# A third chunk's layer norm without TensorE transposes, in a kernel that adds a long convolution to a two-layer MLP

## The chip, the cores and the metric

The kernel runs on one core of a Trainium2 chip. The metric is device time in microseconds; the kernel before took 358.84 us, the median of three runs (358.47 to 358.85). Engines are named as in the profile: PE (TensorE matmuls), PEld (TensorE weight loads), DVE (VectorE), ACT (ScalarE), POOL (GpSimd) and SP (SyncE, here only a queue of DMAs).

## The reference

All tensors have 2048 positions and 448 channels. The input x is layer-normed to xn; the result is x plus two branches.

```python
def A(xn, k, v, shift_k, ssm_k, ssm_D):
    k_shift = sum(k_pad[:, t:t + S] * shift_k[:, 3 - t] for t in range(4))   # causal, 4 taps
    kv = k_shift * v
    y = irfft(rfft(pad(kv), 2 * S) * rfft(pad(ssm_k), 2 * S))[:S]            # long causal convolution
    return xn * (y + kv * ssm_D)

def B(xn, w1, b1, w2):
    h = xn @ w1 + b1                       # 448 -> 1792
    return (h * tanh(softplus(h))) @ w2    # Mish, 1792 -> 448

out = x + A(layernorm(x), k, v, shift_k, ssm_k, ssm_D) + B(layernorm(x), w1, b1, w2)
```

## The kernel before, in words

**The MLP sets the pace.** The 2048 positions are cut into eight chunks of 256. The 1792 hidden channels are seven pairs of 128, so that there are 56 (chunk, pair) items. Item i has two slots of an order that is written out by hand: in slot 2i its first matmul (`g1_mm`, L512, 22 TensorE instructions), and in slot 2i+1 ACT's Mish and its split (`mish`, `split`: L520, L84, L85) together with the second matmul (`g2_mm`, L544 to L546, 12 instructions) of item i-2. Float32 operands are split into a high part, which ACT casts, and a low part, which DVE subtracts: XH and XL for xn, `ach` and `acl` for the activation, `w1h`/`w1l` and `w2h`/`w2l` for the weights. A chunk's two accumulators of the second matmul (`pg2`, two buffers in PSUM, one for each half of the chunk) are added to x by DVE at the chunk's end (`g2_evac`, L551), and only then can the next chunk's second matmul begin.

**The convolution is laid between.** It is a transform in two stages, by small matmuls. In the stretch that the change touches, eight pieces of the kernel of the convolution ("h") and eight of kv go through the first stage: a visit `f1_mm` (L146, PE) reads one piece and writes the PSUM tiles `pq` and `pr`, ACT copies one half to `st` (L152), DVE folds the halves (L156, two instructions) and ACT's queue stores `st` to DRAM (L167). The kv visits stand in slots 24, 29, 34, 39, 44, 50, 55 and 59. Ahead of each, DVE makes the piece from k and v (`taps`: L189, L192, L194 products, L199 sums, L202 the product with v); one product of four is POOL's (L182).

**Layer norm has two forms.** For chunks below NT (0 to 3), `ln_load` and `ln_stats` load x and take mean and variance (L406, L409, L412, POOL's power L415), POOL normalizes (L419, L423), and `ln_T` has PE transpose the result to PSUM (L464, four instructions for each half of a chunk), from which ACT and DVE split it (L476, L474). For chunks from NT on, x is also loaded in a transposed copy (`xT_load`, L434); `nt_stats` stores mean and power to DRAM (L442), `nt_row` (L445) reads them back spread over all partitions, DVE subtracts and multiplies (`nt_norm`, L451, two instructions a half), and `nt_split` (L458, L459) splits from SBUF. The row read back overwrites the identity matrix of the transposes. The table `NT_HOW` gives for each such chunk the slots, counted from the start of the chunk before it, of its load ("q"), transposed load ("x"), statistics, the flush of the statistics, and the rows, norms and splits of its two halves.

**What sets the order.** `at` puts a step in front of a slot's matmuls, `after` behind them. Each engine runs its own instructions strictly in that order, SP's DMA issues too, so that an issue which waits holds up those behind it. Small DVE steps can be put on a list (`drip`) that is taken from between other DVE work, or emptied at once; `ln_T` of a first half empties it.

Of the kernel before, what the change touches and what calls it, by code (L numbers as in the profile page):

```python
# [17 lines left out]
NP = NF // 2  # L18
# [5 lines left out]
G2_LAG = 2  # L24
# [5 lines left out]
I2_AT = {100: ((6, 7, 0, 1), 92, (95, 97, 98, 99), (0, 2, 0, 1)),  # L30
         108: ((2, 3, 4, 5), 101, (104, 105, 106, 107), (0, 1, 0, 1))}
LATE = 2
NT = 4
NT_AT = {"q": -5, "x": -1, "stats": -2, "flush": 0, "row": (4, 8), "norm": (7, 10), "split": (8, 11)}
NT_SOON = dict(NT_AT, row=(4, 5), norm=(4, 7), split=(6, 8))
NT_HOW = {c: NT_SOON for c in (3, 4, 7)}
NT_HOW[5] = dict(NT_AT, q=-8, stats=-4, flush=-2)
WARM_N = (448, 448, 448)
FILL_N = (224, 112, 96)
# [3 lines left out]
def tile_kernel(ctx: ExitStack, tc, q, qT, k, v, sk, hT, sD, w10, w1, w2, c_fib, c_g, c_gi, c_i2, out):  # L43
# [20 lines left out]
    E = dp.tile([NJ * 4, 64, D], F32, name="E")  # L64
    MR = {c: dp.tile([2, CH], F32, name="MR") for c in range(NT, NCHUNK)}

# [8 lines left out]
    def rs(c):  # L75
        return rstd[:, 2 * c:2 * c + 2] if c < NT else mv[:, 2 * c:2 * c + 2, 1]

# [26 lines left out]
    def dv(n=1):  # L104
        for _ in range(n):
            if drip:
                drip.pop(0)()
# [4 lines left out]
    def at(slot, fn, *args):  # L112
        plan.setdefault(int(slot), []).append((fn, args))

    def after(slot, fn, *args):
        plan2.setdefault(int(slot), []).append((fn, args))
# [278 lines left out]
    def xn_tile():  # L395
        return mp.tile([128, 4, CH], F32, name="xn", bufs=1)

    def ln_parts(c):
        st = mp.tile([128, 2, 6], F32, name="bst", bufs=2)
        ve = mp.tile([128, 2], F32, name="ve", bufs=2)  # L400
        if c < NT:
            XN[c] = xn = xn_tile().rearrange("p a b -> p (a b)").rearrange("p (j d) -> p j d", j=2)
        eng = nc.gpsimd if 0 < c < NCHUNK - 1 else V

        def stats(jj):
            V.bn_stats(st[:, jj], Q[c][:, jj])  # L406

        def aggr(jj):
            V.bn_aggr(mv[:, 2 * c + jj], st[:, jj])  # L409

        def eps(a, b):
            V.tensor_scalar(ve[:, a:b], mv[:, 2 * c + a:2 * c + b, 1], EPS, None, op0=ALU.add)  # L412

        def power(a, b):
            nc.gpsimd.tensor_tensor(rs(c)[:, a:b], ve[:, a:b], mhalf[:, a:b], op=ALU.pow)  # L415

        def norm(jj):
            j = 2 * c + jj
            eng.tensor_scalar(xn[:, jj, :D], Q[c][:, jj], mv[:, j, 0:1], rs(c)[:, jj:jj + 1],  # L419
                              op0=ALU.subtract, op1=ALU.mult)  # L420

        def tail(a, b, copy=eng.tensor_copy):
            copy(xn[:, a:b, D:], xn[:, a:b, D - 64:D])  # L423

        return stats, aggr, eps, power, norm, tail, ve
# [52 lines left out]
    def ln_T(c, jj):  # L478
        if jj == 0:
            dv(len(drip))  # L480
            x_tiles(c)
        p = pg()
        transposes(c, jj, p)
        for lo in range(2):
            x_split(c, jj, p, lo)
# [73 lines left out]
    def mlp_slot(s):  # L559
# [3 lines left out]
        if half == 0:  # L563
            if i < n:
                c, p = pairs[i]
                if c + 1 < NT:
                    if p == 0:
# [8 lines left out]
        else:  # L576
            if i < n:
                c, p = pairs[i]
                if p == NP - 2 and c + 1 < NT:
                    ln_T(c + 1, 0)  # L580
# [39 lines left out]
    for p in range(NP):  # L620
        if p >= 3:
            at(max(2 * p - 5, 0), w1_load, p)
        if p == 1 or p > 2:
            at(2 * p - 2, w1_split, p)
        p and at(2 * p + (1 if p < 5 else 0), w2_load, p)
        at(2, w2_split, p) if p == 0 else after(2 * (p + G2_LAG) - 1, w2_split, p)

    at(OCT_AT[0], regroup)
    for o in range(NO):
# [34 lines left out]

    for c in range(NT, NCHUNK):
        at_ = NT_HOW.get(c, NT_AT)
        b = 2 * NP * (c - 1) + (1 if c == NT else 0)
        at(b + at_["q"], ln_load, c)
        at(b + at_["x"], xT_load, c)
        at(b + at_["stats"], nt_stats, c)  # L670
        at(b + at_["flush"], lambda: dv(len(drip)))
        for jj in range(2):
            at(b + at_["row"][jj], nt_row, c, jj)
            after(b + at_["norm"][jj], nt_norm, c, jj)
            after(b + at_["split"][jj], nt_split, c, jj)
# [28 lines left out]
    stats, aggr, eps, power, norm, tail, ve = ln_parts(0)  # L704
# [120 lines left out]
```

## Time and profile before

| | before |
|---|---|
| median of 3 runs | 358.84 us (358.47 to 358.85) |
| profiled execution | 359.38 us |
| its span, first to last instruction | 357.6 us |
| outside the span | 1.78 us |
| granted TensorE clock | 0.998 |
| PE busy | 352.0 us, 98% |
| DVE busy | 269.1 us, 75% |
| ACT busy | 156.8 us, 44% |
| POOL busy | 76.5 us, 21% |

The share of DVE is a mean over unlike stages: from 61.9 to 169.1 us, while the kv pieces are made, it is busy for 103.0 of 107.2 us. The chain that ended last runs through PE for 86% of the span. A row of the timeline gives start, duration, engine, line and operation, and in brackets for how long the engine sat idle before it and what ended that. Instructions of PE and DVE overlap their successors a little, so the time that an instruction costs a queue that never idles is the distance between starts, not the printed duration.

### The profile page before, as it was taken

The numbers are of one execution on the slowest core, as the hardware profiler recorded it, in microseconds if no ns is written. First come the engines' busy times: TensorE is split into PE (matmuls) and PEld (weight loads), VectorE is DVE, ScalarE is ACT, GpSimd is POOL, SyncE is SP. The second block draws the span as 40 slices with busy tenths as digits, with TensorE's granted clock in tenths as the row PEclk, the third lists the DMA queues.
The fourth block names the chain that finished last, engine by engine and source line by source line (L and its number), as shares of the span: only waits on it lengthen the run. The fifth ranks groups of instructions, "written<-read, shape, count | busy, mean of one in ns | idle before, by whom it ended". The sixth has DMA issues, their size and how long they took to land.

```text
span 357.6 us, 7445 instructions
## 1 busy us (share of the span) xinstructions
PE 352.0 (98%) x3100; PEld 290.2 (81%) x3100; DVE 269.1 (75%) x371; ACT 156.8 (44%) x267; POOL 76.5 (21%) x81
## 2 busy tenths in 40 slices
PE   8999999999999999999999999999999999999995
PEld 2988888888888989889997758767775699979795
DVE  5999568999999899899537757756863933788942
ACT  3976643344241542342333453455445343354480
POOL 2037001920128240213000030011031116040030
PEclk9999999999999999999999999999999999999999
DMA  7999978849586446763869569999994386989176
GB/s 242 353 373 303 408 291 221 242 124 285 145 262 217 148 120 169 222 162 82 250 208 353 203 175 295 241 279 310 284 260 131 81 240 252 408 316 284 32 113 144
DMA packets 30227, 82.48 MB, mean 231 GB/s; under 512 B 3057, under 2 KB 15474, under 8 KB 30194
## 3 DMA queue, kind: packets, MB, share of 16 engines
q1 hardware_dynamic: 21410, 47.03, 39.2%
q0 software_dynamic: 4896, 22.95, 22.8%
q10 hardware_dynamic: 3888, 12.03, 12.4%
q8 instruction: 24, 0.39, 0.5%
q14 instruction: 9, 0.07, 0.1%
HBM read 53.55 MB, written 28.45 MB: 229 GB/s over the span
## 4 chain that ended last, share of the span: by engine, by line
PE 86%; DMA 5%; DVE 3%; issue 3%; POOL 2%; SPq 0%; ACT 0%; ACTq 0%; POOLq 0%
PE pg L512 18%; PE pg L544 12%; PE pg L546 12%; PE pg L545 11%; PE pq L512 7%; PE pp L512 5%; PE pr L512 4%; PE pq L146 3%; DMA Dh<-st 3%; PE pp L235 3%; PE pr L235 3%; PE pp L274 2%; DMA kr<-in_w_dram 2%; PE pq L235 2%; PE pr L274 1%
## 5 line engine op out<-in xcount | busy, mean ns | idle before, releaser
L544 PE MATMUL pg<-w2h,ach 128*128 128x448 f32 x224 | 82.4, 368 | 0.0
L545 PE MATMUL pg<-w2l,ach 128*128 128x448 f32 x224 | 81.3, 363 | 0.2 <-DVE w2l L85 0.2
L546 PE MATMUL pg<-w2h,acl 128*128 128x448 f32 x224 | 81.4, 363 | 0.0
L85 DVE TENSOR_TENSOR acl<-a,ach 128x512 fp32r<-128x512 f32 x56 | 38.9, 695 | 32.1 <-ACT ach L84 32.0
L520 ACT ACTIVATE a<-pg,b1t 128x256 f32<-128x256 f32 x66 | 27.8, 472 | 64.3 <-PE pg L512 57.5
L512 PE MATMUL pg<-XH,w1h 128*128 128x256 f32 x264 | 52.7, 283 | 0.0
L544 PEld LDWEIGHTS pg<-w2h,ach 128*128 128x128 f32 x224 | 41.9, 187 | 10.8 <-issue 6.4
L512 PEld LDWEIGHTS pg<-XH,w1h 128*128 128x128 f32 x264 | 41.3, 188 | 6.8 <-issue 6.3
L545 PEld LDWEIGHTS pg<-w2l,ach 128*128 128x128 f32 x224 | 42.1, 188 | 2.9 <-DVE w2l L85 0.5
L546 PEld LDWEIGHTS pg<-w2h,acl 128*128 128x128 f32 x224 | 42.0, 188 | 2.4
L512 PE MATMUL pg<-XL,w1h 128*128 128x256 f32 x264 | 42.9, 277 | 0.0
L156 DVE TENSOR_TENSOR st<-pq,st 128x896 f32<-128x896 f32 x32 | 34.8, 1089 | 5.7 <-ACT st L152 5.0
L512 PEld LDWEIGHTS pg<-XL,w1h 128*128 128x128 f32 x264 | 35.9, 188 | 0.0
L84 ACT CAST ach<-a 128x512 fp32r<-128x512 f32 x56 | 34.8, 622 | 1.7
L512 PE MATMUL pg<-XH,w1l 128*128 128x256 f32 x198 | 33.5, 278 | 0.0
L182 POOL TENSOR_TENSOR x<-kr,skb 128x896 f32<-128x896 f32 x8 | 17.0, 2126 | 71.8 <-DVE x L181 58.6
L512 PEld LDWEIGHTS pg<-XH,w1l 128*128 128x128 f32 x198 | 27.6, 188 | 0.0
L199 DVE TENSOR_TENSOR x<-x 128x896 f32<-128x896 f32 x24 | 26.4, 1100 | 1.0 <-POOL x L182 0.3
L520 ACT ACTIVATE a<-pq,b1t 128x256 f32<-128x256 f32 x20 | 8.4, 471 | 31.8 <-PE pq L512 31.8
L285 POOL DMA_DIRECT2D E<-qe x14 | 8.7, 629 | 63.0 <-ACT qe L282 63.0
L152 ACT COPY st<-pr 128x896 f32<-128x896 f32 x16 | 14.5, 907 | 14.8 <-PE pr L146 12.4
L415 POOL TENSOR_TENSOR mv<-ve,mhalf 128x2 f32<-128x2 f32 x4 | 3.9, 986 | 62.8 <-DVE ve L412 62.8
(138 smaller groups left out, 612.8 us busy)
## 6 DMA issues: line engine op xcount, KB each, us to landing
Dkv<-st ACTq DMA_DIRECT2D x16, 448.0 KB, 6.0
ah<-Dh SPq DMA_DIRECT2D x8, 896.0 KB, 7.7
av<-Dkv SPq DMA_DIRECT2D x8, 896.0 KB, 8.6
e<-E POOLq DMA_DIRECT2D x8, 896.0 KB, 7.4
E<-qe POOLq DMA_DIRECT2D x14, 448.0 KB, 5.9
kr<-in_k_dram SPq DMA_DIRECT2D x10, 448.0 KB, 7.0
Dh<-st ACTq DMA_DIRECT2D x10, 448.0 KB, 6.3
x<-in_hT_dram SPq DMA_DIRECT2D x8, 448.0 KB, 6.8
```

What stands on the lines that cost most here:

```text
L84: nc.scalar.copy(h, raw)
L85: V.tensor_sub(l, raw, h)
L152: nc.scalar.copy(st[:, 1], o)
L156: f(st[:, n], e, st[:, 1])
L182: nc.gpsimd.tensor_mul(o, KR[g - u // 2], skb[:, u:u + 1].to_broadcast([128, 2, D]))
L199: V.tensor_add(KV[g], KV[g], o)
L235: nc.tensor.matmul(p[32 * t:32 * t + 32, r, :D], g[rs, t, c], a[rs, t], start=True, stop=True, tile_position=(64 * r, 32 * t))
L512: nc.tensor.matmul(ps[n], l, r, start=all(m[0] != n for m in seq[:n_]), stop=all(m[0] != n for m in seq[n_ + 1:]))
L520: nc.scalar.activation(a[:, n], ps[n], AF.Mish, bias=b1t[:, 2 * p + n:2 * p + n + 1])
L544: nc.tensor.matmul(ps, ah[:, n, cs], w2h[:, f], start=f == 0, stop=False)
L545: nc.tensor.matmul(ps, ah[:, n, cs], w2l[:, f], start=False, stop=False)
L546: nc.tensor.matmul(ps, al[:, n, cs], w2h[:, f], start=False, stop=f == NF - 1)
```

## The change

Chunk 3 takes the second form of layer norm, so that only chunks 1 and 2 are still transposed inside the loop. Its x is loaded in front of slot 20 (before: 28), its statistics are listed in front of slot 25 (before: slot 34, spread over what followed), its transposed copy is loaded in slot 28, its rows are read in slots 33 and 34, its norms stand behind the matmuls of slots 33 and 36, and its splits behind those of 35 and 37. In slot 25 the list is emptied at once by `ln_T` of chunk 2, so the statistics and the store of chunk 3's row run there in one piece. The sixth piece of w2 is split in front of slot 12 and no longer behind slot 13. In the line with `b`, chunk 4 keeps the offset that it had.

```diff
-NT = 4
+NT = 3
-NT_HOW = {c: NT_SOON for c in (3, 4, 7)}
+NT_HOW = {c: NT_SOON for c in (4, 7)}
+NT_HOW[3] = dict(NT_SOON, q=-9, stats=-4, flush=-3)
@@
-        at(2, w2_split, p) if p == 0 else after(2 * (p + G2_LAG) - 1, w2_split, p)
+        if p in (0, 5):
+            at(2 if p == 0 else 12, w2_split, p)
+        else:
+            after(2 * (p + G2_LAG) - 1, w2_split, p)
@@
-        b = 2 * NP * (c - 1) + (1 if c == NT else 0)
+        b = 2 * NP * (c - 1) + (1 if c < 5 else 0)
```

The order on DVE around slots 33 and 34 before: the last sum of the third piece's first taps, the fold of the visit in slot 34 (`st`), with chunk 3's statistics between.

```order
L199 TENSOR_TENSOR x<-x 128x896
L181 MEMSET x 1x1
L156 TENSOR_TENSOR st<-pq,st 128x896
L406 BN_STATS bst<-qt 128x6
L156 TENSOR_TENSOR st<-pq,st 128x896
L406 BN_STATS bst<-qt 128x6
L409 BN_AGGR mv<-bst 128x2
L199 TENSOR_TENSOR x<-x 128x896
```

The same place in the changed kernel, where line numbers are higher by one. `xn` is chunk 3's transposed copy, `con` holds the row read back, and the MEMSET is what releases POOL's product.

```order
L200 TENSOR_TENSOR x<-x 128x896
L452 TENSOR_TENSOR xn<-xn,con 128x4x128 x2
L182 MEMSET x 1x1
L157 TENSOR_TENSOR st<-pq,st 128x896 x2
L200 TENSOR_TENSOR x<-x 128x896
```

The two norm instructions stand in front of the fold, and the statistics are gone from here. They are now in slot 25, behind the last sum with POOL's product and in front of chunk 2's split:

```order
L200 TENSOR_TENSOR x<-x 128x896
L407 BN_STATS bst<-qt 128x6 x2
L410 BN_AGGR mv<-bst 128x2 x2
L413 TENSOR_SCALAR ve<-mv 128x2
L475 TENSOR_TENSOR XL<-pg_942,XH 128x4x128
```

On SP's queue of DMAs before, behind the store of chunk 0's MLP part (`out_dram`): an h piece, k and v of the second kv piece.

```order
L557 DMA out_dram<-qt 128x896
L132 DMA x<-in_hT_dram 128x896
L172 DMA kr<-in_k_dram 128x896
L176 DMA x<-in_v_dram 128x896
L172 DMA kr<-in_k_dram 128x896
```

In the changed kernel chunk 3's load of x stands directly behind that store, whose buffer it takes, and so waits until the store has landed; the three other loads stand behind it.

```order
L558 DMA out_dram<-qt 128x896
L391 DMA qt<-in_q_dram 128x896
L133 DMA x<-in_hT_dram 128x896
L173 DMA kr<-in_k_dram 128x896
L177 DMA x<-in_v_dram 128x896
```

On ACT the cast of w2's sixth piece (`w2h<-x`) stood behind slot 13's Mish:

```order
L84 CAST w2h<-kr 128x896
L476 CAST XH<-pg_539 128x4x128
L152 COPY st<-pr 128x896
L520 ACTIVATE a<-pg_546,b1t 128x256 x2
L84 CAST ach<-a 128x512
L84 CAST w2h<-x 128x896
```

and now follows the fifth piece's cast at once:

```order
L85 CAST w2h<-kr 128x896
L85 CAST w2h<-x 128x896
L477 CAST XH<-pg_542 128x4x128
L153 COPY st<-pr 128x896
```

## The prediction

> **What bounds the kernel now.** I read the page's busy times and chain first.
>
> ```profile
> PE 352.0 (98%) x3100; PEld 290.2 (81%) x3100; DVE 269.1 (75%) x371; ACT 156.8 (44%) x267; POOL 76.5 (21%) x81
> ...
> PE 86%; DMA 5%; DVE 3%; issue 3%; POOL 2%; SPq 0%; ACT 0%; ACTq 0%; POOLq 0%
> ```
>
> PE is the bound, and what the change can give is PE time: transposes left out, and a wait. The chain of waits prices the transposes, PE's timeline the wait.
>
> ```profile
> 115.48 0.59 PE pg L464 x4
> ...
> 118.48 0.44 PE pg L464 x4
> ```
> ```profile
> 45.95 0.36 PE L544 MATMUL pg<-w2h,ach 128*128 128x448 f32 x1
> ...
> 46.50 0.47 PE L545 MATMUL pg<-w2l,ach 128*128 128x448 f32 x1 [0.19 <-DVE w2l L85]
> ...
> 46.81 0.36 PE L546 MATMUL pg<-w2h,acl 128*128 128x448 f32 x1
> 47.01 0.36 PE L544 MATMUL pg<-w2h,ach 128*128 128x448 f32 x1
> ```
>
> Chunk 3's two groups of transposes hold 0.59 + 0.44 = 1.03 us of the chain. In slot 15 these matmuls follow each other at 0.20 us (46.81 to 47.01); L546 starts 0.86 us behind L544 where two steps would be 0.40, so the late w2l costs 0.46 us. Together 1.49 us: the most that I find on PE.
>
> The next question is whether DVE lets PE keep that. DVE makes the kv pieces almost without a pause. Its timeline:
>
> ```profile
> 61.93 1.09 DVE L156 TENSOR_TENSOR st<-pq,st 128x896 f32<-128x896 f32 x1 [1.09 <-ACT st L152]
> ...
> 103.07 1.09 DVE L156 TENSOR_TENSOR st<-pq,st 128x896 f32<-128x896 f32 x1
> ...
> 106.21 1.06 DVE L199 TENSOR_TENSOR x<-x 128x896 f32<-128x896 f32 x1
> ...
> 110.24 1.49 DVE L202 TENSOR_TENSOR x<-x 128x896 f32<-128x896 f32 x1
> ...
> 114.48 1.33 DVE L199 TENSOR_TENSOR x<-x 128x896 f32<-128x896 f32 x1
> 116.73 0.69 DVE L474 TENSOR_TENSOR XL<-pg,XH 128x512 fp32r<-128x512 f32 x1 [0.92 <-ACT XH L476]
> 118.12 0.69 DVE L85 TENSOR_TENSOR acl<-a,ach 128x512 fp32r<-128x512 f32 x1 [0.70 <-ACT ach L84]
> ...
> 128.13 0.62 DVE L406 BATCH_NORM_STATS2 bst<-qt 128x6 f32<-128x448 f32 x1
> 128.67 0.30 DVE L409 BATCH_NORM_AGGREGATE mv<-bst 128x2 f32<-128x6 f32 x2
> ...
> 129.08 0.69 DVE L85 TENSOR_TENSOR acl<-a,ach 128x512 fp32r<-128x512 f32 x1
> ...
> 134.66 1.08 DVE L199 TENSOR_TENSOR x<-x 128x896 f32<-128x896 f32 x1
> 135.67 1.14 DVE L551 TENSOR_TENSOR qt<-pg,qt 128x448 f32<-128x448 f32 x2
> ...
> 140.65 1.41 DVE L451 TENSOR_TENSOR xn<-xn,con 128x512 f32<-128x512 f32 x2
> 141.98 1.08 DVE L189 TENSOR_TENSOR x<-kr,skb 128x896 f32<-128x896 f32 x1
> 143.77 0.69 DVE L85 TENSOR_TENSOR acl<-a,ach 128x512 fp32r<-128x512 f32 x1 [0.71 <-ACT ach L84]
> ...
> 146.58 0.68 DVE L459 TENSOR_TENSOR XL<-xn,XH 128x512 fp32r<-128x512 f32 x1
> 147.19 1.09 DVE L156 TENSOR_TENSOR st<-pq,st 128x896 f32<-128x896 f32 x1
> ...
> 149.56 1.09 DVE L199 TENSOR_TENSOR x<-x 128x896 f32<-128x896 f32 x1 [0.16 <-POOL x L182]
> ...
> 167.98 1.09 DVE L202 TENSOR_TENSOR x<-x 128x896 f32<-128x896 f32 x1
> ```
>
> At 61.93 DVE waits for PE's visit, and then only at 116.73, 118.12 and 143.77: these pauses are all the slack it has until the last kv piece is ready at 167.98 + 1.09 = 169.07. PE needs DVE at two tight places, slot 47 (chunk 3's second matmul takes over the accumulators that L551 empties from 135.67) and slot 59 (the last kv visit):
>
> ```profile
> 137.14 0.36 PE L544 MATMUL pg<-w2h,ach 128*128 128x448 f32 x1
> ...
> 169.12 0.59 PE L146 MATMUL pq<-x,con 32*64 32x448 f32 x2
> ```
>
> In slot 59 PE starts 0.05 us behind the piece it reads: there both engines are already level. In slot 47 the first accumulator is free at about 135.67 + 1.14/2 = 136.24, 0.9 us ahead.
>
> **The change part by part.** *w2's sixth piece sooner* takes the 0.46 us away if its raw data are there and nothing behind it becomes late.
>
> ```profile
> 28.40 0.42 SPq L379 DMA_DIRECT2D x<-in_w_dram  x1
> ```
> ```profile
> x<-in_w_dram SPq DMA_DIRECT2D x1, 448.0 KB, 5.8
> ```
> ```profile
> 36.67 0.94 ACT L84 CAST w2h<-kr 128x896 fp32r<-128x896 f32 x1
> 38.73 0.59 ACT L476 CAST XH<-pg 128x512 fp32r<-128x512 f32 x1 [1.12 <-PE pg L464]
> ```
>
> The load lands at 28.40 + 5.8 = 34.2; ACT idles 1.12 us from 37.6, so a cast of 0.94 us hides in front of XH. On DVE the subtraction (128x896, like L156 some 1.1 us) would run from 38.6 to 39.7, and chunk 1's last XL, which needs the cast at 38.73 to end at 39.3, starts some 0.4 us later; its first reader stands in slot 14, the slot in front of the L544 at 45.95. If that cover were gone, PE would wait these 0.4 us instead of the 0.46. Gain 0.46 us, from slot 15 on, DVE's start at 61.93 included.
>
> *The transposes* give PE 1.03 us more in slots 39 and 40. Their splits (L476, L474) are replaced by as many from SBUF (L458, L459), at no cost: the XL at 116.73, from PSUM, took 0.69 us and that at 146.58, from SBUF, 0.68, with 147.19 - 146.58 = 0.61 us to the next start. POOL loses its normalization.
>
> *DVE's path from 61.9*, relative to before:
> - It starts 0.46 us earlier.
> - The statistics in slot 25 add 0.54 + 0.54 + 0.41 = 1.49 us (two L406 steps of 128.67 - 128.13; from 128.67 to 129.08 the rest).
> - In slot 34 they are gone. The stretch from the fold to the next sum took 106.21 - 103.07 = 3.14 us, and two small steps behind it some 0.27 (three took 0.41); without statistics a fold and its sum take 149.56 - 147.19 = 2.37, POOL's product included. That returns 1.04 us, less than was paid, since the statistics had filled the wait for POOL.
> - Four norm steps: 141.98 - 140.65 = 1.33 us a half, 2.66 in all, one half ahead of the fold of slot 34, one behind the third piece.
> - Steps slowed by POOL's normalization become normal: L202 at 110.24 by 1.49 - 1.09 = 0.40.
> - The pauses at 116.73 and 118.12 close. From 114.48 to 116.73 stand 2.25 us where L199 takes 1.01 (135.67 - 134.66), and to 118.12 another 1.39 where XL takes 0.61: 1.24 + 0.78 = 2.02 us.
>
> Sum: -0.46 + 1.49 - 1.04 + 2.66 - 0.40 - 2.02 = +0.23 at 119 us; I take +0.2 (between 0 and 0.4, for small waits that the distances of starts hide). While PE comes 1.49 us earlier, DVE in slot 47 comes 0.2 us later: the first accumulator is free at 136.44, PE would be there at 135.65. PE waits 0.8 us and starts at some 136.5, 0.6 us earlier than before instead of 1.5. At 143.77 the pause of 0.71 closes as well, and DVE is 0.2 - 0.71 = -0.5 us: the last kv piece is ready at 168.6, and slot 59 starts 0.5 us earlier than before. What is left of 1.49 us is **0.5 us**; from there PE, ACT and the loads all follow slot 59, and I carry 0.5 to the end.
>
> Here a page speaks against the norm's new place. POOL's power (L415) for chunk 3 runs in slot 25, beside DVE's splits, which read two operands.
>
> ```profile
> 129.25 1.09 POOL L415 TENSOR_TENSOR mv<-ve,mhalf 128x2 f32<-128x2 f32 x1 [8.21 <-DVE ve L412]
> ```
>
> For chunk 4 the L85 at 129.08 ran beside it in its usual 0.69 us, so I charge nothing. The Trainium skill, "SBUF — State Buffer", section "Who interferes with whom", says that a VectorE instruction with two SBUF inputs contends with a GpSimd instruction that reads SBUF, and that the later one fully blocks; by that rule the split would wait up to 1.09 us, and the sum would be a loss of 0.6 us. This trace doesn't show it at this place; at 110.24, beside a longer POOL instruction, it shows a stretch by 0.40 only.
>
> *SP's queue.* Chunk 3's load of x waits for the store of chunk 0 to land, and three loads wait behind it.
>
> ```profile
> 56.98 0.35 SPq L557 DMA_DIRECT2D out_dram<-qt  x1
> ...
> 58.67 1.08 SPq L172 DMA_DIRECT2D kr<-in_k_dram  x1
> ```
> ```profile
> out_dram<-qt SPq DMA_DIRECT2D x1, 448.0 KB, 4.7
> ```
> ```profile
> kr<-in_k_dram SPq DMA_DIRECT2D x1, 448.0 KB, 7.0
> ```
> ```profile
> 69.86 1.08 DVE L189 TENSOR_TENSOR x<-kr,skb 128x896 f32<-128x896 f32 x1
> ```
>
> The store lands at 56.98 - 0.46 + 4.7 = 61.2. Then x, h and k are issued, k at about 62.2 instead of 58.67. With the 7.0 us that it took before, again behind two transfers, it lands at 69.2; the product that reads it would start at 69.86 - 0.46 = 69.4. That is 0.2 us of cover. The store's 4.7 us bounds it from below; from above, a later k load in a crowd:
>
> ```profile
> kr<-in_k_dram SPq DMA_DIRECT2D x1, 448.0 KB, 7.9
> ```
>
> With 7.9 us it lands at 70.1 and DVE pauses 0.7 us, which goes straight through to slots 47 and 59. I take no pause. The second row's read-back (L445) waits for the first norm at about 105.4 and now stands in front of the fifth piece's k load, whose product starts at about 115.3; with 7.9 us k lands at 113.8. No cost.
>
> **Sum.** The profiled execution took 359.38 us, its span 357.6 and 1.78 around it, which I take as unchanged; 359.38 - 0.5 = 358.9. It lay 0.54 us above the median of the three runs, so against 358.84 the forecast is 358.3.
>
> **The rivals.**
> 1. *PE keeps most of it*, because DVE has 0.3 to 1 us more slack than I count (my sum of starts was rounded by 0.2, and all of POOL's relief isn't in it: L199 at 114.48 was stretched as well). For it: each of the pauses shows DVE waiting. Against: slot 59 has 0.05 us between the engines. Up to 1.49 us: 357.35; a middle case 357.8.
> 2. *The second k load is late* (slower). DVE stands still at 69.4, with the next activation's split queued behind the product. From a landing at 69.4 + 0.5 = 69.9 the gain is gone, from 70.6 on it is a loss of over 0.7 us. The 7.9 us row gives 70.1, 358.3 + 0.7 = 359.0; as much again beyond it as lies between the two rows (an estimate) gives 71.0 and 359.9.
> 3. *The fold in front of slot 34 or the read-back is late.* The norm's new work stands in front of folds and of the fifth piece; a row that lands 3 us late would idle DVE by about 1 us: 359.3. For it: the row's read starts only when the first norm is done. Against: the second norm stands some 8 us behind the first.
> 4. *The page's block*: 359.4, on the other side of no change by 0.6.
> That the freed PE time reappears as waits is the forecast itself.
>
> **How the numbers follow.** About 0.2% (0.7 us) is what a measurement of this kernel can tell from no change. Forecast 0.42, of which 0.06 beyond 0.7 us of gain; rival 1 0.27, faster; rival 2 0.18, of which 0.10 over 0.7 us slower; rival 3 0.09, of which 0.05 slower; rival 4 0.04, within. Faster 0.06 + 0.27 = 0.33; slower 0.15; the rest, 0.52, within. The likeliest case's own range is 358.0 to 358.6. The whole range goes from rival 1's end, 357.4, to 359.5, and leaves out part of rivals 2 and 3.
>
> **What the profile after would show.** No wait of PE for w2l in slot 15, L545 0.20 us behind L544. No L464 behind 80 us. DVE without pauses from 61.5 to about 168 us; PE waiting about 0.8 us for L551 in slot 47 and little or up to 1 us in all for L202 in slot 59. The second k load landing by 69.4, and no pause of DVE in front of that L189. A pause there, or a stretched split beside POOL's power, would make the prediction wrong on the slow side; slot 59 starting over 1 us earlier, on the fast side.

## The result, and the profile after

The changed kernel takes 360.03 us (median of 8 runs, 359.20 to 361.02) against 358.83 us (median of 8, 358.47 to 359.08): 1.0036 times the time before, with a 95% interval of 1.0026 to 1.0045. It is slower by 1.2 us, where 358.3 was forecast. The profiled execution took 359.85 us with a span of 358.1 us.

The page's busy times and its chain, after:

```profile
PE 351.5 (98%) x3092; PEld 289.4 (81%) x3092; DVE 270.9 (76%) x375; ACT 156.7 (44%) x267; POOL 70.1 (20%) x78
...
PE 91%; DVE 5%; ACT 1%; issue 1%; DMA 1%; POOL 1%; POOLq 0%
```

PE has 0.5 us less to do and DVE 1.8 us more, and DVE's share of the chain is 5% (3% before). PE's timeline after, at the places of which the prediction speaks, and at one of which it doesn't:

```profile
48.04 0.59 PE L147 MATMUL pq<-x,con 32*64 32x448 f32 x2
...
78.44 0.61 PE L513 MATMUL pg<-XH,w1h 128*128 128x256 f32 x3 [0.36 <-DVE XL L475]
...
137.20 0.44 PE L545 MATMUL pg<-w2h,ach 128*128 128x448 f32 x1 [0.88 <-ACT a L521]
...
169.28 0.59 PE L147 MATMUL pq<-x,con 32*64 32x448 f32 x2
```

The first row is the visit of slot 16, the last that of slot 59. Between them stand two waits that the kernel before didn't have. The one in slot 47 was forecast (0.8 us). The profile puts it down to ACT's `a` here, which happens to end at 137.19; in e4, a second trace of the same kernel, PE starts at 137.02 while that step of ACT runs to 137.16, and there, in e9 and in e10 the wait is put down to L552. The wait in slot 26 wasn't forecast. DVE's timeline after:

```profile
76.23 1.15 DVE L407 BATCH_NORM_STATS2 bst<-qt 128x6 f32<-128x448 f32 x2
77.29 0.30 DVE L410 BATCH_NORM_AGGREGATE mv<-bst 128x2 f32<-128x6 f32 x2
...
77.70 0.69 DVE L475 TENSOR_TENSOR XL<-pg,XH 128x512 fp32r<-128x512 f32 x1
...
87.73 1.09 DVE L200 TENSOR_TENSOR x<-x 128x896 f32<-128x896 f32 x1
89.54 0.69 DVE L86 TENSOR_TENSOR acl<-a,ach 128x512 fp32r<-128x512 f32 x1 [0.71 <-ACT ach L85]
...
136.44 1.14 DVE L552 TENSOR_TENSOR qt<-pg,qt 128x448 f32<-128x448 f32 x2
...
168.13 1.09 DVE L203 TENSOR_TENSOR x<-x 128x896 f32<-128x896 f32 x1
```

The statistics hold DVE from 76.23 to 77.70, 1.47 us, and XL behind them frees the PSUM tile that PE wants at 78.1 in slot 26. At 89.5 DVE pauses for ACT. ACT's timeline there says why:

```profile
82.12 0.62 ACT L85 CAST ach<-a 128x512 fp32r<-128x512 f32 x1
85.06 2.90 ACTq L168 DMA_DIRECT2D Dh<-st  x2
88.02 0.84 ACT L521 ACTIVATE a<-pg,b1t 128x256 f32<-128x256 f32 x2 [5.28 <-DVE x L195]
```

The issue of two stores takes 2.90 us; Mish stands behind it and starts at once when it ends.

**Most of the loss lies in front of slot 59, the rest at the very end.** From that visit to the last L552 there are 184.87 us in this trace (354.15 - 169.28) and 184.88 in that of before (354.00 - 169.12), so nothing is lost between. From the last L552 to the end of the span, however, there are 3.95 us (358.1 - 354.15) and 3.60 before (357.6 - 354.00). The last store lands 2.58 us behind the start of that L552 in both; what differs is how many of the waits with which SP closes the program (each for two semaphores, nearly all of them DMAs', some 0.06 us apart) still follow. The waits behind this landing, before and then after:

```profile
L820 SPq EVENT_SEMAPHORE  x3: 28/28/28, 356.6 to 356.7; - x3
```
```profile
L824 SPq EVENT_SEMAPHORE  x8: 28/28/28, 356.7 to 357.2; - x8
```

These waits come in the same order in both kernels, but the last store signals another semaphore, one that comes sooner in their order, so that five more of them follow its landing: 0.31 us. All traces agree: from the last L552 to the end of the span pass 3.88 to 4.06 us in the 14 in which chunk 3 has its second form, and 3.57 to 3.73 in the six in which it has its first.

The visits of slots 26 to 59, counted from that of slot 16, are the measure of every experiment below; the 0.3 us at the end come on top wherever chunk 3 has its second form (us; all from PE's timelines, first row of each visit):

| kernel | 26 | 29 | 34 | 44 | 50 | 59 | median, ratio to before (95%) |
|---|---|---|---|---|---|---|---|
| before, first trace | 28.45 | 37.50 | 52.10 | 79.76 | 95.63 | 120.21 | 358.83 |
| before again, e5 | 28.45 | 37.50 | 52.10 | 79.76 | 95.64 | 120.21 | one run, 358.85 |
| w2's split alone, e1 | 28.44 | 37.49 | 52.10 | 79.76 | 95.63 | 120.20 | 358.78, 1.0001 (0.9992 to 1.0009) |
| after | 28.45 | 38.00 | 52.71 | 79.65 | 96.65 | 121.24 | 360.03, 1.0036 (1.0026 to 1.0045) |
| after again, e4 | 28.44 | 38.01 | 52.61 | 79.55 | 96.41 | 120.97 | one run, 359.74 |
| chunk 3 alone, e2 | 28.44 | 38.00 | 52.67 | 79.61 | 96.58 | 121.16 | 360.32, 1.0046 (1.0033 to 1.0058) |
| no norm, e3 | 28.44 | 38.00 | 52.65 | 79.58 | 95.46 | 120.02 | 358.81, 0.9997 (0.9988 to 1.0006) |
| statistics late, e6 | 28.45 | 37.50 | 53.24 | 80.16 | 97.09 | 121.66 | 360.31, 1.0040 (1.0027 to 1.0053) |
| xT later, e7 / e11 | 28.45 | 38.10 / 38.18 | 52.71 | 79.65 | 95.82 / 96.34 | 120.40 / 120.93 | 359.86, 1.0023 (1.0013 to 1.0033) |
| norm on POOL, e8 | 28.45 | 37.99 | 54.53 | 81.45 | 97.87 | 122.45 | 361.50, 1.0072 (1.0053 to 1.0091) |
| small store later, e9 | 28.45 | 38.00 | 52.61 | 79.55 | 95.84 | 120.42 | 359.22, 1.0008 (0.9999 to 1.0017) |
| and statistics behind, e10 | 28.45 | 37.55 | 52.16 | 79.10 | 95.85 | 120.43 | 359.38, 1.0014 (1.0005 to 1.0023) |
| before with a small store, e12 | 28.45 | 37.49 | 52.10 | 79.76 | 95.63 | 120.20 | 358.93, 1.0001 (0.9992 to 1.0010) |
| L552 sooner, e13 | 28.44 | 38.11 | 52.72 | 79.65 | 95.68 | 120.99 | 359.98, 1.0030 (1.0021 to 1.0040) |
| e10 and e13, e14 | 28.45 | 37.63 | 52.24 | 79.18 | 95.05 | 120.33 | 359.25, 1.0012 (1.0004 to 1.0021) |
| before, L551 sooner, e15 | 28.44 | 37.49 | 52.09 | 79.76 | 95.63 | 120.20 | 359.19, 1.0009 (0.9999 to 1.0018) |
| e14, products sooner, e16 | 28.45 | 37.50 | 52.10 | 79.04 | 94.92 | 120.08 | 358.94, 1.0005 (0.9996 to 1.0014) |
| after, products sooner, e17 | 28.45 | 37.84 | 53.21 | 80.16 | 97.12 | 121.69 | 360.56, 1.0041 (1.0027 to 1.0056) |
| before, products sooner, e18 | 28.44 | 37.49 | 52.10 | 79.76 | 95.63 | 120.19 | 358.92, 0.9993 (0.9981 to 1.0004) |

Row "after" against row "before": 0.50 lost from slot 26 to 29, 0.11 more up to 34, 0.72 gained by the transposes from 34 to 44, 1.13 lost in front of slot 50 (the wait in slot 47), together 1.03 us. The visits lose more than the idle times in the rows, 0.36 us in slot 26 and 0.88 in slot 47; where the rest of the 0.50 and 1.13 arises is not taken apart here.

### The profile page after: what moved, and what is told of

Read it like the earlier page. It is cut to its first block, busy times and chain, and to the rows that moved or that the text cites. A ratio compares the mean times of both kernels' runs of the same rounds, so it can differ in the third digit from the quotient of the medians.

```text
span 358.1 us, 7433 instructions
## 1 busy us (share of the span) xinstructions
PE 351.5 (98%) x3092; PEld 289.4 (81%) x3092; DVE 270.9 (76%) x375; ACT 156.7 (44%) x267; POOL 70.1 (20%) x78
## 3 DMA queue, kind: packets, MB, share of 16 engines
HBM read 54.34 MB, written 28.45 MB: 231 GB/s over the span
## 4 chain that ended last, share of the span: by engine, by line
PE 91%; DVE 5%; ACT 1%; issue 1%; DMA 1%; POOL 1%; POOLq 0%
PE pg L513 21%; PE pg L545 13%; PE pg L547 12%; PE pg L546 12%; PE pq L513 7%; PE pp L513 5%; PE pr L513 4%; PE pq L147 3%; PE pp L236 3%; PE pr L236 3%; PE pp L275 2%; PE pq L236 2%; PE pr L275 1%; PE pp L329 1%; DVE x L200 1%
## 5 line engine op out<-in xcount | busy, mean ns | idle before, releaser
L545 PE MATMUL pg<-w2h,ach 128*128 128x448 f32 x224 | 82.6, 369 | 0.9 <-ACT a L521 0.9
L546 PE MATMUL pg<-w2l,ach 128*128 128x448 f32 x224 | 81.2, 363 | 0.0
L86 DVE TENSOR_TENSOR acl<-a,ach 128x512 fp32r<-128x512 f32 x56 | 38.9, 695 | 32.4 <-ACT ach L85 32.1
L545 PEld LDWEIGHTS pg<-w2h,ach 128*128 128x128 f32 x224 | 41.9, 187 | 12.6 <-issue 8.2
L546 PEld LDWEIGHTS pg<-w2l,ach 128*128 128x128 f32 x224 | 42.1, 188 | 2.4
L200 DVE TENSOR_TENSOR x<-x 128x896 f32<-128x896 f32 x24 | 26.2, 1092 | 1.3 <-POOL x L183 0.7
L416 POOL TENSOR_TENSOR mv<-ve,mhalf 128x2 f32<-128x2 f32 x5 | 4.7, 933 | 64.9 <-DVE ve L413 64.8
```

What stands on the lines that cost most here:

```text
L86: V.tensor_sub(l, raw, h)
L200: V.tensor_add(KV[g], KV[g], o)
L545: nc.tensor.matmul(ps, ah[:, n, cs], w2h[:, f], start=f == 0, stop=False)
L546: nc.tensor.matmul(ps, ah[:, n, cs], w2l[:, f], start=False, stop=False)
```

## The experiments

### Which part loses: e1, e2, e4 and e5

Each half of the change alone, and both kernels a second time. e1:

```diff
 (before)
-        at(2, w2_split, p) if p == 0 else after(2 * (p + G2_LAG) - 1, w2_split, p)
+        if p in (0, 5):
+            at(2 if p == 0 else 12, w2_split, p)
+        else:
+            after(2 * (p + G2_LAG) - 1, w2_split, p)
```

> The kernel before with one change: w2's sixth piece is split in slot 12; chunk 3 keeps its transposes. Theory A (what the change lost lies in chunk 3's new path over VectorE, and the sooner split is worth the 0.46 us that slot 15's wait lost): 358.83 - 0.46 = about 358.4. Theory B (the sooner split itself costs time further on, for instance by moving the later transfers into each other): 358.8 or more, up to 359.5. In the profile by A: no wait of TensorE for w2l in slot 15, the kv visits earlier by 0.4 to 0.5 us up to the end.

e2 is the changed kernel with these lines put back:

> The changed kernel with w2's sixth piece split behind slot 13 as before; only chunk 3's layer norm is changed. Theory A (chunk 3's path loses, the split gains): 360.03 + 0.46 = about 360.5. Theory B (the sooner split is what loses): 359 or less. If TensorE's wait in slot 47 for the accumulators swallows whatever comes before it, as the profile after suggests, then VectorE starts 0.46 us later and both the wait's end and the time move with it, which is again A's number.

> The changed kernel itself, for a second trace. Theory A (fixed work on VectorE): TensorE's waits in slots 26 (about 0.4 us, for the split of chunk 2), 47 (about 0.9 us) and the kv visits lie as in the first trace within 0.2 us. Theory C (transfers that crowd): the issue of the store of Dh by ScalarE near 85 us (2.9 us in the first trace, 1.24 before) and the waits behind it differ by 0.5 us or more, and the time with them.

> The kernel before, for a second trace. Theory D (the wait of 0.46 us for w2l in slot 15 was a chance of the one execution that I read; it is missing in the trace of the changed kernel with w2's split put back, 11.35 us between the visits on either side of it against 11.81): no wait there, 11.35 us, and a profiled time near 358.7. Against it (the wait is part of the kernel before): 11.8 us again, with 359.2 to 359.4.

Chunk 3 alone loses (e2, 1.0046), but w2's split alone gains nothing: 358.78 against 358.73 in the same runs. Theory A missed e1 by 0.4 us and B is not needed for it. That e2 comes near A's 360.5 is luck: it has no wait in slot 15 either, and reaches slot 59 as the changed kernel does (121.16 against 121.24). The second trace of before shows what happened. PE's timeline in slot 15 of e5:

```profile
45.85 0.36 PE L544 MATMUL pg<-w2h,ach 128*128 128x448 f32 x1
46.05 0.36 PE L545 MATMUL pg<-w2l,ach 128*128 128x448 f32 x1
46.25 0.36 PE L546 MATMUL pg<-w2h,acl 128*128 128x448 f32 x1
```

L546 stands 0.40 us behind L544; nothing waits for w2l. Between the visits of slots 12 and 16 lie 11.34 us here, 11.81 in the first trace. Of the six traces in which w2 is split behind slot 13, two have the wait (11.81 before, 11.96 in e12) and four don't (11.34 or 11.35 in e2, e5, e15 and e18). D holds: the 0.46 us were an accident of the execution that the prediction read.

In e4 the changed kernel's waits lie as in its first trace (0.35 us in slot 26, 0.74 in slot 47), with an issue of 2.72 us on ACT. So they belong to the kernel.

### Is it VectorE's path: e3

```diff
 (after)
-            after(b + at_["norm"][jj], nt_norm, c, jj)
+            if c != 3:
+                after(b + at_["norm"][jj], nt_norm, c, jj)
```

> The changed kernel without the two subtract-and-multiply instructions of each half of chunk 3 (four in all): chunk 3's input of the MLP is left unnormalized, everything else stays. VectorE's path from slot 33 on is 2.66 us shorter. Theory A (VectorE's path decides at slots 47 and 59): TensorE's wait in slot 47 goes, slot 59 starts up to 1.5 us earlier, 357.9 to 358.8. Theory C (slow issues of transfers and waits for PSUM buffers between 76 and 92 us decide): little change, 359.3 or more, since TensorE's own losses in front of slot 34 stay.

358.81, at the slow end of A's range. PE's wait in slot 47 is gone, and all 1.2 us of the loss with it, while the 0.5 us in slot 26 stay (38.00 in the table). DVE's path decides, and what PE loses ahead of slot 34 alone would not have made the kernel slower.

### What slows ScalarE's issue: e7, e11, e9 and e12

First suspect: the transposed load, which runs beside four other transfers.

```diff
 (after)
-NT_HOW[3] = dict(NT_SOON, q=-9, stats=-4, flush=-3)
+NT_HOW[3] = dict(NT_SOON, q=-9, stats=-4, flush=-3, x=2)
```

> The changed kernel with chunk 3's transposed copy loaded in slot 31 instead of 28, behind the loads of k and v that follow it. Theory F (ScalarE's slow issue of the store near 85 us comes from that transfer's company): the issue takes about 1.24 instead of 2.8 us, VectorE's pause of 0.5 to 0.7 us at 89.5 goes, slot 47 and the time come 0.5 to 0.7 us earlier, 359.3 to 359.5. Against it: the issue stays at 2.5 us or more, 360.0.

> The kernel with the later transposed load for a second trace, since the profiled execution of the first (358.99) was the fastest of ten (median 359.86). If the fast execution was a chance of the transfers: about 359.8 with ScalarE's issue near 85 us above 2 us, or a pause of VectorE elsewhere of 0.7 us or more. If the profile is right and the others differ by something that only shows without a profile: about 359.0 again, with an issue of 1.24 us.

Theory F's 359.3 to 359.5 was missed (359.86). In the first trace ACT's issue took 1.24 us, but SP's issue of the moved load took 3.16, and the other nine runs of that kernel took 359.70 to 360.39 against the trace's 358.99. In the second trace (359.96) ACT's issue took 2.62 us and DVE paused 0.42. Moving this load moves the slow issue about; it doesn't take it away.

Second suspect: GpSimd's store of mean and power, 2 KB, which the change put among these transfers.

```diff
 (after)
-                     lambda: (eps(0, 2), power(0, 2), nt_store(c))])
+                     lambda: (eps(0, 2), power(0, 2), c != 3 and nt_store(c))])
...
+    at(31, nt_store, 3)
```

> The changed kernel with GpSimd's store of chunk 3's mean and power moved from slot 25 to slot 31, out of the time in which seven large transfers run. Theory G (this store of 2 KB slows the transfers beside it, so that ScalarE's issue of the store near 85 us takes 2.8 us): the issue falls to 1.24 us, the k load at 79.55 lands in 8 us or less instead of 9.0, VectorE's pause at 89.5 goes, TensorE waits 0.1 us at most in slot 47: 359.0 to 359.2. Against it: issue of 2.5 us or more, 360.0.

The reverse, in the kernel before (MX is a place in DRAM that nobody reads):

```diff
 (before)
+    def tiny_store():
+        V.tensor_copy(mv[:, 14:16], mv[:, 4:6])
+        for _ in range(2):
+            nc.gpsimd.tensor_tensor(mv[:, 14:16, 1], mv[:, 14:16, 1], mhalf, op=ALU.pow)
+        nc.gpsimd.dma_start(MX.rearrange("j (p t) -> p j t", t=2), mv[:, 14:16])
+
+    at(25, tiny_store)
```

> The kernel before with a small store of its own: a copy of eight bytes by two per partition of chunk 2's statistics on VectorE in slot 25, two powers on GpSimd, and a store of 2 KB to a place that nobody reads, issued near 78.5 us. Theory G: the transfers beside it get slower, ScalarE's issue near 84 us takes 2.4 us or more instead of 1.24 and VectorE pauses 0.5 us or more behind it; slot 47's slack of 0.9 us covers this, so the time stays at 358.7 to 359.1. Against G: the issue stays at 1.24 us and nothing pauses.

ACT's timeline of e9, then of e12:

```profile
85.00 1.24 ACTq L168 DMA_DIRECT2D Dh<-st  x2
86.29 0.84 ACT L521 ACTIVATE a<-pg,b1t 128x256 f32<-128x256 f32 x2 [3.62 <-PE pg L513]
```
```profile
84.20 2.81 ACTq L167 DMA_DIRECT2D Dh<-st  x2
87.06 0.84 ACT L520 ACTIVATE a<-pg,b1t 128x256 f32<-128x256 f32 x2 [4.23 <-DVE x L194]
```

DVE's timeline of e12, and that kernel's DMA issues from 78 to 92 us (KB, median us from issue to landing):

```profile
88.58 0.69 DVE L85 TENSOR_TENSOR acl<-a,ach 128x512 fp32r<-128x512 f32 x1 [0.62 <-ACT ach L84]
```
```profile
Dkv<-st ACTq DMA_DIRECT2D x2, 448.0 KB, 8.9
...
MX<-mv POOLq DMA_DIRECT2D x1, 2.0 KB, 8.6
```

G holds from both sides. Without the small store the changed kernel's issue takes 1.24 us, DVE doesn't pause, and the time falls to 359.22. With it the kernel before has the issue of 2.81 us and the pause of 0.62, and its stores land after 8.9 us (6.4 in e5). That kernel's time doesn't change, since DVE has slack there, as expected. All 20 traces together: the issue takes 1.24 us in each of the ten without a small store near 79 us, and 2.62 to 2.90 in eight of the ten with it. The other two are e7, where SP's issue of 3.16 us stands in its place, and e17 (below), where no issue is slow.

### The statistics' place: e6 and e10

```diff
 (after)
-NT_HOW[3] = dict(NT_SOON, q=-9, stats=-4, flush=-3)
+NT_HOW[3] = dict(NT_SOON, q=-9)
```

> The changed kernel with chunk 3's statistics listed in slot 27 instead of 25 and spread over what follows instead of emptied at once. Theory A (VectorE's path decides in slot 47, whatever TensorE loses in front of it): TensorE's wait in slot 26 for chunk 2's split goes and the visit of slot 29 comes 0.5 us earlier, but the wait in slot 47 grows by as much: 359.6 to 360.1. Theory E (the burst is the cause of the loss): 359.4 or less. If the store of ScalarE near 85 us was slowed by the store of mean and power, its issue falls from 2.8 to about 1.24 us and VectorE, and the time, gain 0.5 to 0.7 us.

e10 is e9 with `stats=-3, flush=-3`:

> The same, and chunk 3's statistics one slot later, behind chunk 2's first split and the third piece's product with v instead of in front of them. By theory A with G, TensorE's wait in slot 26 (0.5 us) goes too, and VectorE reaches slot 47 some 0.8 us later than in the kernel before, against 0.9 us of slack there: 358.6 to 358.9, within the measurement of the kernel before. If something else bounds the stretch: 359.3 or more.

In both, the wait in slot 26 goes (37.50 and 37.55 in slot 29). In e6 (360.31, A had said 359.6 to 360.1) it comes back twofold, because the power and the small store now stand in front of POOL's product; DVE's timeline of e6:

```profile
88.29 0.16 DVE L413 TENSOR_SCALAR ve<-mv 128x2 f32<-128x2 f32 x1
...
92.94 1.09 DVE L200 TENSOR_TENSOR x<-x 128x896 f32<-128x896 f32 x1 [1.76 <-POOL x L183]
```

In e10 nothing is late but DVE itself. Its L552 and PE's L545 behind it:

```profile
135.82 1.14 DVE L552 TENSOR_TENSOR qt<-pg,qt 128x448 f32<-128x448 f32 x2
```
```profile
136.58 0.44 PE L545 MATMUL pg<-w2h,ach 128*128 128x448 f32 x1 [0.64 <-DVE qt L552]
```

PE comes 0.5 us sooner than in e9 and waits 0.5 us longer; both reach slot 59 at 120.4. I had expected 358.6 to 358.9 and got 359.38. PE starts 0.76 us behind L552's start here, in e9 (135.56 and 136.32) and in the changed kernel (136.44 and 137.20). In the kernel before it started 1.47 us behind (135.67 and 137.14). The slack there was thus 0.71 us, not 0.9.

### Slot 47 or slot 59: e13, e14 and e15

```diff
 (after; before in e15; e10 in e14)
-        if s % 2 == 0 and j >= 0 and pairs[j][1] == NP - 1:
+        if s % 2 == 0 and j >= 0 and pairs[j][1] == NP - 1 and s != 46:
             g2_evac(pairs[j][0])
...
         mlp_slot(s)
+        if s == 45:
+            g2_evac(2)
```

> The changed kernel with the emptying of chunk 2's accumulators (L552) one step sooner in VectorE's order: in front of the sum of POOL's product behind the fold of slot 44, not behind it. VectorE's total stays. Theory A (in slot 47 TensorE waits for L552 by its place in VectorE's order, and nothing behind it binds): L552 starts 1.0 us sooner, the wait of 0.88 us goes, all that follows comes 0.9 us sooner: 359.1. If the sum that is now later, or the last kv visit (slot 59), binds in its place: 359.7 or more.

> The changed kernel with all three: the small store in slot 31, the statistics one slot later, L552 one step sooner. By theory A with G nothing is left of the waits in slots 26 and 47 and of the slow issue, and the transposes' 0.7 us stay with TensorE: 0.4 to 0.6 us below the kernel before, 358.2 to 358.4. If a further wait takes their place: 358.8 or more.

> The kernel before with L551 one step sooner. There it was ready 0.7 us ahead of TensorE, so theory A expects no change: 358.7 to 358.9. A gain of 0.3 us or more would say that the kernel before waited there already.

The wait in slot 47 goes and slot 50 comes 0.97 us sooner (95.68 against 96.65), but the time stays at 359.98. PE's timeline of e13, then of e14:

```profile
169.29 0.59 PE L147 MATMUL pq<-x,con 32*64 32x448 f32 x2 [0.71 <-DVE x L203]
```
```profile
168.71 0.59 PE L147 MATMUL pq<-x,con 32*64 32x448 f32 x2 [0.67 <-DVE x L203]
```

So theory A in the form "slot 47 alone" fell: what PE saves there it waits for the last kv piece in slot 59. Not one hand-over decides but DVE's whole path from 61 us on, which ends in two places at nearly the same lateness. e14 shows the rest: with none of the waits in slots 26 and 47 and no slow issue, slot 59 still comes at 120.33, by DVE, and the time is 359.25, not 358.2 to 358.4; of the 0.45 us to the kernel before (358.80 in the same runs) 0.31 are those at the end. The control e15 reaches slot 59 as before; its median of 359.19 lies above the 358.7 to 358.9 that were expected, but is not told from no change (0.9999 to 1.0018).

### The norm on another engine: e8

```diff
 (after)
-            V.tensor_tensor(x, x, m, op=op)
+            (nc.gpsimd if c == 3 else V).tensor_tensor(x, x, m, op=op)
```

> The changed kernel with chunk 3's four subtract-and-multiply steps on GpSimd instead of VectorE. Theory A (VectorE's 2.66 us of these steps are what TensorE waits for in slot 47): as without the steps, 358.8, if GpSimd's steps don't slow VectorE; each of the four, at about 1.2 us by GpSimd's 2.13 us for 896 elements, may stretch a VectorE step beside it by 0.4 us, together 1.6 us at most, of which TensorE would wait for about 0.5: 359.3 then. Against A: 359.7 or more.

361.50, the slowest of all: POOL's steps cost DVE more than its own had. The timelines of POOL and of DVE in e8:

```profile
93.82 3.01 POOL L452 TENSOR_TENSOR xn<-xn,con 128x512 f32<-128x512 f32 x2 [1.45 <-DMA con<-MR]
...
108.68 3.43 POOL L452 TENSOR_TENSOR xn<-xn,con 128x512 f32<-128x512 f32 x2
```
```profile
93.42 0.62 DVE L193 TENSOR_TENSOR x<-kr,skb 128x448 f32<-128x448 f32 x1
93.96 1.72 DVE L195 TENSOR_TENSOR x<-kr,skb 128x448 f32<-128x448 f32 x1
95.71 2.08 DVE L200 TENSOR_TENSOR x<-x 128x896 f32<-128x896 f32 x1
...
108.77 2.18 DVE L200 TENSOR_TENSOR x<-x 128x896 f32<-128x896 f32 x1
110.87 1.80 DVE L86 TENSOR_TENSOR acl<-a,ach 128x512 fp32r<-128x512 f32 x1
```

Each of the four POOL steps lengthens the DVE step beside it by 1.0 to 1.1 us (L195 from 0.62, L200 from 1.09, L86 from 0.69), 4.3 us in all for 2.66 us freed. The Trainium skill, "SBUF — State Buffer", section "Who interferes with whom", says that a VectorE instruction with two SBUF inputs and a GpSimd instruction that reads SBUF exclude each other. Here the trace agrees: steps of 1.5 to 1.7 us on POOL, 1.0 to 1.1 us lost beside each.

### DVE's path made shorter without leaving work out: e16, e17 and e18

```diff
 (e14 in e16, after in e17, before in e18)
+    def taps_early(g, u):
+        PP[g, u] = o = xt()
+        V.tensor_mul(o[:, 0], KR[g - (u + 1) // 2][:, 1], skb[:, u])
+        V.tensor_mul(o[:, 1], KR[g - u // 2][:, 0], skb[:, u])
...
         at(t, f1_mm, HT, g, "h")
+        if t == 20:
+            at(t, taps_early, 0, 3)
```

> The changed kernel with the three edits before (small store in slot 31, statistics one slot later, L552 one step sooner) and a fourth: the two products of the first kv piece's last tap (0.53 us each) stand in front of the fold of slot 20, in the 1.1 us for which VectorE waits there, instead of behind it. VectorE's path from 61.4 us on is 1.07 us shorter. Theory A (both tight places, slots 47 and 59, are set by this path): no wait of TensorE in slots 26, 47 and 59, the transposes' 0.66 us stay: slot 59 at 119.5 to 119.6 us behind the visit of slot 16 (120.2 in the kernel before), 358.1 to 358.3. If the gain is again turned into a wait elsewhere: 358.7 or more.

> The changed kernel with the fourth edit alone. Theory A: VectorE's path is 1.07 us shorter in slots 47 and 59, so TensorE's wait of 0.88 us in slot 47 goes and slot 59 comes 0.8 to 0.9 us sooner; its 0.5 us in slot 26 may stay or go, since VectorE comes 1 us sooner there as well: 358.7 to 359.2. If the path is not what decides: 359.8 or more.

> The kernel before with the fourth edit alone, the control. There TensorE waited for VectorE neither in slot 47 nor, but for 0.05 us, in slot 59, so theory A expects 358.6 to 358.9, no change.

The products fill the pause at 61.4, but DVE keeps little of the 1.07 us. DVE's timeline of e16, and POOL's:

```profile
62.17 1.33 DVE L418 TENSOR_SCALAR ve<-mv 128x2 f32<-128x2 f32 x1
...
73.57 1.09 DVE L157 TENSOR_TENSOR st<-pq,st 128x896 f32<-128x896 f32 x1
75.15 1.09 DVE L205 TENSOR_TENSOR x<-x 128x896 f32<-128x896 f32 x1 [0.49 <-POOL x L183]
```
```profile
61.34 2.13 POOL L183 TENSOR_TENSOR x<-kr,skb 128x896 f32<-128x896 f32 x1 [27.42 <-ACT st L153]
...
64.42 4.26 POOL L425 TENSOR_SCALAR xn<-qt,mv,rstd 128x448 f32<-128x448 f32 x1
...
73.00 2.12 POOL L183 TENSOR_TENSOR x<-kr,skb 128x896 f32<-128x896 f32 x1
```

The first of it goes at once. The marker that releases a POOL product now stands behind the moved products, so that this product runs from 61.34 to 63.47, and DVE's small step L418 between the two folds ends only with it, at 63.50: 1.33 us instead of 0.20 in e14 (e17 and e18 show the same, 1.32 and 1.26 us). More goes at 73 us. Without the edit (e14) DVE's marker releases the POOL product there; now POOL itself is late with chunk 2's normalization (the step at 64.42 took 4.26 us, 2.77 in e14). The product starts 24.86 us behind slot 16's visit instead of 25.02, and DVE waits 0.49 us for it (0.17 in e14). What remains is 0.25 us (slot 59 at 120.08 against 120.33). e16 is level with the kernel before, 358.94 against 358.93, instead of 358.1 to 358.3; it reaches slot 59 0.13 us sooner than that kernel and loses 0.31 at the end. e17 took 360.56 instead of 358.7 to 359.2. It has the small store in its old place; there ACT waits 2.25 us for a store of kv to land and DVE's fold 1.61 us for ACT. That the small store causes this too is likely, but not shown. e18 is the control, without change. No version beat the kernel before by what can be measured.

## Why the prediction was wrong

The faulty step is the sum of **DVE's path** ("-0.46 + 1.49 - 1.04 + 2.66 - 0.40 - 2.02 = +0.23"): one term in it doesn't exist in most executions, and one is missing, the slow issue of ACT's store. Behind it a second step failed: the end of the program was taken as unchanged. Against an ordinary execution of before (e5), at slot 59:

| | predicted | measured |
|---|---|---|
| start of DVE's path sooner, by w2 | -0.46 | 0 (e1, e5) |
| its other terms up to 119 us and L552 | +0.69 | +0.84 (e9: L552 87.59 us behind slot 16's visit, e5 86.75) |
| pause at 143.77 closes | -0.71 | -0.71 (none in DVE's timeline after) |
| slow issue of ACT's store | 0 | +0.82 (after against e9: 121.24 - 120.42; +0.55 with e4's 120.97) |
| not assigned | 0 | +0.08 |
| sum | -0.48 | +1.03 |

Point by point:

- *w2's sixth piece.* The wait of 0.46 us was real in the row, but it occurs in some executions only, two of six traces. The prediction said that the profiled execution of before lay 0.54 us above the median, and then took a gain that contains this wait off the median of 358.84, where there is mostly no such wait to gain.
- *The transposes* were taken at 0.59 + 0.44 = 1.03 us from the chain's durations. The table shows 0.72 (27.66 against 26.94 us from slot 34 to 44). The distances of starts would have said it; PE's timeline before:

```profile
115.42 0.66 PE L464 MATMUL pg<-con,xn 128*128 128x128 f32 x4
115.83 0.45 PE L544 MATMUL pg<-w2h,ach 128*128 128x448 f32 x1
...
118.32 0.60 PE L464 MATMUL pg<-con,xn 128*128 128x128 f32 x4
118.68 0.60 PE L512 MATMUL pg<-XH,w1h 128*128 128x256 f32 x3
```

0.41 + 0.36 = 0.77 us.
- *The statistics* were right in size (1.47 against 1.49) but their place was looked at for DVE only. XL behind them holds a PSUM tile that PE needs in slot 26: 0.5 us. It cost nothing in the end, because PE would have waited that much longer in slot 47 (e9 against e10).
- *The row's store.* The prediction followed the loads on SP's queue one by one; the 2 KB store on POOL's queue was not priced. It is what made ACT's issue slow, and it is the largest missed term. Rivals 2 to 4 had lateness near the right place, but not this one: the second k load landed in time (no pause of DVE in front of its L190), the fold was not late by the read-back, and the split beside POOL's power took its usual time (L86 at 78.30, 0.68 us, power from 77.87 to 78.58).
- *Slot 47.* The wait was forecast at 0.8 us and is 0.88, which is luck. Counted from slot 16's visit, L552 was to come 0.69 us later than before and PE 1.03 sooner; L552 came 1.65 later (88.40 against 86.75) and PE 0.11 sooner (slot 44). And PE starts 0.76 us behind L552's start, not half of 1.14.
- *Slot 59* within 0.05 us of DVE was right: e13 and e14 show the wait there as soon as slot 47 is relieved.
- *The end.* The prediction carried 0.5 us from slot 59 to the end and took what lies behind as unchanged. Up to the last L552 that held (184.87 and 184.88 us); behind the last store's landing 0.31 us were lost.

**What stays open.** 1.03 us up to slot 59 and 0.31 at the end make 1.34, where the medians are 1.20 apart; the difference is not taken apart. Single executions scatter by more: PE reaches the visit of slot 12 anywhere from 36.61 to 37.12 us in the 20 traces. By what rule the last store gets its semaphore was not looked into. In e7 nine runs were 0.7 to 1.4 us slower than the traced one; that they had the slow issue is likely by e11, but not seen. By what means a 2 KB store slows the issue and the landing of others was not tried: from 79.5 to 84.5 us the core's DMAs moved 341 GB/s with it and 351 without (e12 and e5), so the total that they moved hardly fell.

## What to carry to other kernels

Before a wait in a profile is counted as a gain, see whether the execution is an ordinary one: a profile 0.5 us above its kernel's median may hold a wait that most executions lack, and a second trace of the unchanged kernel shows it. Compare the ends of the two spans as well, behind the last store. Where two engines are level, sum the whole path of the one that gets work, up to each hand-over, and count a moved step's smallest DMA too, by what transfers it now runs beside. Work taken from the bound engine is worth its distance of starts, and only as far as the engine beside it has slack, here 0.71 us.

## What the runs showed of the hardware

- A store of 2 KB issued by POOL among transfers of 448 KB made the issue of two stores on ACT's queue take 2.62 to 2.90 us instead of 1.24 (eight traces of ten, after and e12 among them) and landed itself after 8.8 and 8.6 us (after, e12); out of the crowd it landed after 3.4 (e9). The Trainium skill, "DMA: Bandwidth & Descriptors", section "Rules for kernel authors", says that transfers under 64 KB pay mostly overhead; the runs show a price for their neighbours as well.
- An issue that is slow holds up its engine's arithmetic: 2.90 us on ACT became a pause of 0.71 us on DVE, and some 0.8 us on PE (after against e9).
- DVE's steps with both operands in SBUF lose 1.0 to 1.1 us beside a POOL step with two operands (e8); DVE's folds, which read one operand from PSUM, took 1.08 and 1.09 us beside POOL's product of 2.12 us (e16). How short a POOL step may be to cost nothing is open: beside POOL's power of 0.71 us the split L86 kept its 0.68 us (after).
- SP's closing waits for DMA semaphores stand 0.06 us apart. With eight of them behind the last landing the span ends 0.31 us later than with three.
